# A second set of buffers for k, q and v of every other late pair, and weight sums at other slots

## The chip, the cores and the metric

The kernel runs on one core of a Trainium2 chip. The metric is the device time of one execution in microseconds (us). The kernel before took 863.57 us, the median of three timed runs (862.11 to 866.70). One further execution was profiled; times within the program are from that one and count from the start of its span.

The engines are named as the profile names them: PE multiplies matrices (PEld loads its weights), DVE works on vectors, ACT applies functions and copies, and SP issues nearly all DMAs. Each engine runs its instructions in program order and waits on semaphores for the others.

## The reference

Windowed attention, then a feed-forward layer, all in fp32:

```
q, k, v: [8, 8, 576, 64]                      # batch, heads, sequence, head size
s = (q @ k.T) / 8, masked                     # heads 0-3: the last 32 keys
                                              # heads 4-7: 32 keys, every 4th of the last 128
a = exp(s - max(s));  a = a / (sum(a) + 1e-9)
x = (a @ v), heads side by side               # [4608, 512]: 8 * 576 tokens
h = x @ w_in                                  # [4608, 2048]
g = max(h, 0) + alpha * min(h, 0)
out = g @ w_out                               # [4608, 512]
```

## The kernel before, in words

**Attention.** The 8 x 8 heads are worked as 32 pairs of heads, numbered p = 4 * batch + c; the name 6_1 is batch 6, c = 1, so pair 25. A `Pair` loads k, q and v (L216, L217, L224), multiplies scores on PE (L268), takes row maxima on DVE (L296, L299), exponentials on ACT (L309), divisions and a transpose on DVE (L316 to L324), multiplies values on PE (L286), and copies the result to its place on ACT (L393, `highs`) and DVE (L400, `lows`). Pairs 0 to 19 run in the first 346 us. The twelve late pairs, 20 to 31, run between the matmuls of the paired stage below. Each has one tile for k, one for q and one for v, of which the pool `att` holds one buffer each.

**Feed-forward.** The 4608 tokens are 9 tiles of 512. An fp32 product is made of three products of high and low parts. Tiles 0 to 2 are done singly, early. Tiles 3 to 8 are done two at a time from `paired_stage` (L1109): `phase_h` makes half of h for both tiles by seven block products in place of eight (class `Four`), and `phase_y` (L889) multiplies that half with w_out, in 32 slots of 12 matmuls each (slot n = 8 * column block + row block). A stage is named (t - 3, half): (0, 0) and (0, 1) are tiles 3 and 4, (2, 0) and (2, 1) tiles 5 and 6. Where a stage is listed in `SEVENS` the output product, too, is made of seven block products, which need sums of blocks of w_out.

**Hooks.** What other engines do in a `phase_y` hangs on its slots: a dictionary from slot to operations, which are issued after that slot's matmuls. `attention_hooks` puts pair k of the stage at slots 3 + 5k (scores, the next pair's k and q, maxima, exponentials), 4 later (division, transpose) and 8 later (values, the next pair's v, copies; 7 later for the last). In stage (0, 0) these are pairs 21 to 25; the end of pair 20 is at slot 5.

**Weight sums.** `second_sums` hangs eight sets of sums of w_out blocks on the slots by the table `SUMS`: for each set its number, the slots of its four fetches (256 KB each, from wO into the tiles wy), the slot of its sums on DVE (L1055 and four of L1058), the slot of its parts (a cast on ACT, L1062; a subtraction on DVE, L1063; two stores of 512 KB to wY, L1065, issued by SP), and the pair of buffers. Buffers 1 and 2 hold sets with last entry 1, buffers 3 and 4 those with 3; set 2 thus fetches into the buffers of set 0, and set 7 into those of set 5. Buffers 1 to 4 are also the `stage` tiles of the next `phase_h` (L723, L730).

**Weights.** Every weight block of the paired stage goes through a ring of 10 slots of 256 KB. `feed` (L623) loads the next block each time a slot is used; at every third call it first runs one entry of the list `waiting`, which before the change holds only eight loads of kept tokens. These ring loads, the fetches, the stores, the pairs' loads and the outputs stand in SP's order as the program issues them.

Of the kernel before, what the change touches and what calls it, by code (L numbers as in the profile page):

```python
# [8 lines left out]
F32 = mybir.dt.float32  # L9
# [8 lines left out]
P = 128  # L18
B, H, S, D = 8, 8, 576, 64
# [10 lines left out]
TT = 512  # L30
# [38 lines left out]
def tile_window_attention_prelu_ffn(  # L69
# [12 lines left out]
    nc = tc.nc  # L82
    PS = bass.MemoryType.PSUM

    const = ctx.enter_context(tc.tile_pool(name="const", bufs=1))
# [14 lines left out]
    sums = [const.tile([P, HB], F32, name=f"sums{i}") for i in range(2)]  # L100
# [4 lines left out]
    wY = dram.tile([NFP, 4, P, 2, 2 * P], F32, name="wY")  # L105
    kept = {t: dram.tile([NC, P, TT], F32, name=f"kept_{t}") for t in KEPT}

    turn = {"a": 0, "y": 0, "g": 0, "i": 0, "f": 0}
# [6 lines left out]
    def gbuf(shape, dtype, name, i=None):  # L115
        if i is None:
            i = turn["g"] % 5
            turn["g"] += 1
        return ffp.tile(shape, dtype, tag=f"g{i}", name=name, bufs=1)
# [28 lines left out]
    vsize = (HB + 1) * D  # L148
# [8 lines left out]
    cells = {}  # L157
# [18 lines left out]

    class Pair:
        def __init__(self, b, c):  # L180
            self.b, self.c = b, c
            p = b * NC + c
            self.onto = p <= NC + 1
            self.banks = "y" if self.onto else "a"
            self.late = p == 0
            self.plain = 2 * c < HP
            self.mask = PLAIN if self.plain else DILATED
            self.id = f"{b}_{c}"
            self.pr = spare_pr[p % 2] if b < 2 else pr0
            self.room = rooms[c] if b < 2 else None  # L190
            self.sm = sums[p % 2]
            self.mixed = p >= AHEAD
            self.sides = None
            self.kept = {}

        def target(self, t):
# [11 lines left out]

        def load_qk(self):
            b, c = self.b, self.c  # L210
            if self.room is None:
                self.k = att.tile([P, S], F32, tag="k", name=f"k_{self.id}")
                self.q = att.tile([P, S], F32, tag="q", name=f"q_{self.id}")
            else:
                self.k, self.q = self.room[:, :S], self.room[:, S:2 * S]
            nc.sync.dma_start(out=self.k, in_=kT[b, c])  # L216
            nc.sync.dma_start(out=self.q, in_=qT[b, c])  # L217

        def load_v(self):
            if self.room is None:  # L220
                self.v = att.tile([P, HB + 1 + self.mixed, D], F32, tag="v", name=f"v_{self.id}")
            else:
                self.v = self.room[:, 2 * S:taken].rearrange("p (j d) -> p j d", d=D)
            nc.sync.dma_start(out=self.v, in_=vX[self.b - AHEAD // NC, self.c] if self.mixed else vW[self.b, self.c])  # L224
# [386 lines left out]
    ring, fed, used, waiting = {}, [0], [0], []  # L611
# [10 lines left out]

    def feed():  # L623
        turn["f"] += 1
        if waiting and turn["f"] % 3 == 0:
            waiting.pop(0)()
        if fed[0] < len(units):
            to, u = slot(fed[0]).bitcast(F32), units[fed[0]]
            nc.sync.dma_start(out=to if len(u.shape) == 2 else to.rearrange("p (c n) -> p c n", c=2), in_=u)
            fed[0] += 1  # L630
# [5 lines left out]
    parts, stage = {}, {}  # L636
# [293 lines left out]
    def seven_y(t, grp, us, hooks):  # L930
# [100 lines left out]
                op()  # L1031

    SUMS = {
# [4 lines left out]
    }  # L1038

    def second_sums(hooks, at):  # L1040


        for i, first, then, last, k in SUMS.get(at, ()):
            room = {}

            def fetch(j, i=i, k=k, room=room):
                a, odd = j // 2, j % 2
                if j == 0:
                    room["x"], room["t"] = (gbuf([P, 2, NC, P], F32, f"wy{i}_{n}", k + n) for n in range(2))
                nc.sync.dma_start(  # L1050
                    out=room["xt"[a]][:, odd], in_=wO[i // GP, :, i % GP, :, odd, a].rearrange("c p n -> p c n"))

            def sums(room=room):
                x, t = (room[a].rearrange("p o c n -> p (o c n)") for a in "xt")
                nc.vector.tensor_tensor(out=t, in0=x, in1=t, op=ALU.add)  # L1055
                t = t.rearrange("p (q n) -> p q n", q=4)
                for out, x, y, op in ((3, 1, 3, ALU.add), (1, 0, 1, ALU.subtract), (0, 3, 0, ALU.subtract), (2, 2, 0, ALU.subtract)):
                    nc.vector.tensor_tensor(out=t[:, out], in0=t[:, x], in1=t[:, y], op=op)  # L1058

            def parts(i=i, room=room):  # L1060
                x, t = (room[a].rearrange("p o c n -> p (o c n)") for a in "xt")
                nc.scalar.copy(out=x.bitcast(F32R), in_=t)  # L1062
                nc.vector.tensor_tensor(out=t.bitcast(F32R), in0=t, in1=x, op=ALU.subtract)  # L1063
                for a, w in enumerate((x, t)):
                    nc.sync.dma_start(  # L1065
                        out=wY[i, :, :, a].rearrange("q p n -> p q n"), in_=w.rearrange("p (q n) -> p q n", q=4))

            for j, n in enumerate(first):
                hooks.setdefault(n, []).append(lambda j=j, fetch=fetch: fetch(j))
            for n, op in ((then, sums), (last, parts)):  # L1070
                hooks.setdefault(n, []).append(op)

    def first_scores(u):
        u.scores()
        if u is not pairs[-1]:
            pairs[pairs.index(u) + 1].load_qk()
        u.maxima()

    def begin(u):
# [11 lines left out]
    def end(u):  # L1091
        def op():
            u.values()
            if u is not pairs[-1]:
                pairs[pairs.index(u) + 1].load_v()
            u.highs()
            u.lows()
            u.keep()
        return op
# [9 lines left out]
    def paired_stage():  # L1109
        todo = pairs[AHEAD:]  # L1110
        for u in todo:
            u.banks = "a"
        for t in range(NSTD, NTILE, 2):
            for grp in range(NFP // GP):
                hooks, early = {}, None
# [13 lines left out]
                if t == NSTD:  # L1129
                    early, us, todo = todo[0], todo[1:6], todo[6:]  # L1130
                last = phase_h(t, grp, early=early)[-1]
# [24 lines left out]
    pairs = [Pair(b, c) for b in range(B) for c in range(NC)]  # L1156
# [12 lines left out]
    def conversion():  # L1169

        w = Conversion(*convs.pop(0))
        w.magnitude()
        return w
# [29 lines left out]
    w = conversion()  # L1203
# [5 lines left out]
    before, w = w, conversion()  # L1209
    for s in range(NC):  # L1210
        u = pairs[s]
# [27 lines left out]
        before, w = w, later  # L1239
# [10 lines left out]
    u, v = pairs[NC - 1], pairs[NC]  # L1250
# [70 lines left out]
    for p in range(2 * NC, AHEAD):  # L1321
        n = EARLY + 2 * (p - 2 * NC)
# [5 lines left out]
    for k in range(NFP):  # L1328
        n = SCRATCH + 1 + 2 * k + (2 if k > 1 else 0)
# [89 lines left out]
    feed()  # L1419
    feed()  # L1420
    paired_stage()


# [66 lines left out]
```

## Time and profile before

| what | us |
|---|---|
| median of three runs | 863.57 (862.11 to 866.70) |
| profiled execution | 860.51 |
| its span in the trace | 858.4 |
| PE busy | 838.6 (98%) |
| DVE busy | 615.9 (72%) |
| ACT busy | 433.9 (51%) |
| DMA | 183.48 MB, 214 GB/s over the span |

Busy time is the sum of an engine's instructions. A row of the chain of waits gives a start, a duration and what filled it: an instruction, a DMA on its way, or "issue" where the profile shows nothing that was waited for. A row of a timeline gives start, duration, engine (SPq is SP's queue of DMA issues, with the time to issue and not to land), line, and output and input tile. Granted clock 1.00 is the full TensorE clock.

### The profile page before, as it was taken

The page shows a single profiled execution, that of the slowest core. Times are in us where ns is not written, and L with a number is a line of the kernel's source. Part 1 is how long each engine was busy: PE and PEld are TensorE (multiplying, and loading weights), DVE is VectorE, ACT ScalarE, POOL GpSimd, SP SyncE. Part 2 cuts the span into 40 slices and gives each one's busy share as a digit, 9 for nine tenths or more (in the row PEclk, how much of TensorE's full clock was granted, in tenths as well). Part 3 has the DMA queues.
Part 4 walks back from the last instruction along what each step waited for, and adds up shares of the span by engine and source line. Part 5 has one row for each costly group of instructions (what it writes and reads, how often), then busy time and mean ns, then how long its engine had stood idle before and what let it go on. Part 6 is the DMA issues. An engine that isn't in the chain of part 4 may idle for free.

```text
span 858.4 us, 20273 instructions
## 1 busy us (share of the span) xinstructions
PE 838.6 (98%) x8118; PEld 681.8 (79%) x8118; DVE 615.9 (72%) x1061; ACT 433.9 (51%) x1206; POOL 46.9 (5%) x52
## 2 busy tenths in 40 slices
PE   8789999999999999999999999999999989999998
PEld 5567888888888888887788877888888868888886
DVE  5987767676776768786757788688376758944893
ACT  7885766434344444565437555465265216534640
POOL 0000000200505340000000000000000000000000
PEclk9999999999999999999999999999999999999999
DMA  7743344126989964767987577867886987676664
GB/s 259 266 169 112 138 159 148 44 93 189 293 260 327 314 217 157 237 185 230 304 292 203 176 241 242 269 195 237 257 256 197 286 270 207 191 196 196 191 190 158
DMA packets 133626, 183.48 MB, mean 214 GB/s; under 512 B 10654, under 2 KB 75806, under 8 KB 133534
## 3 DMA queue, kind: packets, MB, share of 16 engines
q1 hardware_dynamic: 133534, 182.20, 67.7%
q8 instruction: 64, 1.05, 0.5%
q14 instruction: 28, 0.23, 0.1%
HBM read 138.12 MB, written 44.04 MB: 212 GB/s over the span
## 4 chain that ended last, share of the span: by engine, by line
PE 91%; DMA 4%; DVE 3%; issue 1%; SPq 0%; ACT 0%; DVEq 0%; ACTq 0%
PE h L466 16%; PE y L514 15%; PE pA L681 15%; PE y L889 11%; PE pC L681 8%; PE qA L1025 7%; PE pB L681 4%; PE qC L1025 4%; PE o L339 3%; PE s L244 2%; PE qB L1025 2%; DMA wy<-wO 2%; PE o L286 1%; PE s L268 1%; DMA w_dt.float<-qT 1%
## 5 line engine op out<-in xcount | busy, mean ns | idle before, releaser
L466 PE MATMUL h<-x,w_dt.float32r 128*128 128x512 f32 x576 | 142.3, 396 | 0.9 <-ACT x L393 0.8
L514 PE MATMUL y<-g,w_dt.float32r 128*128 128x512 f32 x576 | 138.3, 389 | 0.0
L466 PEld LDWEIGHTS h<-x,w_dt.float32r 128*128 128x128 f32 x576 | 107.9, 190 | 24.2 <-ACT x L393 0.9
L514 PEld LDWEIGHTS y<-g,w_dt.float32r 128*128 128x128 f32 x576 | 107.9, 188 | 22.5
L309 ACT ACTIVATE pr<-pr,nm 128x64 f32<-128x64 f32 x216 | 72.3, 337 | 65.6 <-DVE nm L299 65.6
L723 ACT COPY stage<-pA 128x512 f32<-128x512 f32 x72 | 42.0, 584 | 65.9 <-PE pA L681 62.4
L492 ACT CAST g<-m 128x512 fp32r<-128x512 f32 x48 | 29.7, 619 | 74.8 <-DVE m L487 68.7
L681 PE MATMUL pA<-parts_w,ring_w 128*128 128x512 f32 x234 | 58.1, 390 | 3.2 <-ACT stage L723 3.2
L889 PE MATMUL y<-gp,ring_xA 128*128 128x512 f32 x252 | 60.7, 395 | 0.0
L889 PE MATMUL y<-gp,ring_w 128*128 128x512 f32 x240 | 58.2, 394 | 0.0
L681 PE MATMUL pA<-parts_w,ring_xA 128*128 128x512 f32 x234 | 57.8, 389 | 0.0
L889 PEld LDWEIGHTS y<-gp,ring_xA 128*128 128x128 f32 x252 | 46.5, 188 | 10.1
L681 PEld LDWEIGHTS pA<-parts_w,ring_w 128*128 128x128 f32 x234 | 43.8, 188 | 12.7 <-ACT stage L723 3.6
L889 PEld LDWEIGHTS y<-gp,ring_w 128*128 128x128 f32 x240 | 44.3, 188 | 9.6
L681 PEld LDWEIGHTS pA<-parts_w,ring_xA 128*128 128x128 f32 x234 | 43.9, 188 | 9.2
L497 DVE TENSOR_TENSOR g<-m,g 128x512 fp32r<-128x512 f32 x48 | 33.6, 700 | 15.6 <-ACT g L492 15.5
L730 DVE TENSOR_TENSOR stage<-pC,stage 128x512 f32<-128x512 f32 x48 | 33.0, 688 | 12.7 <-ACT stage L723 12.3
L486 DVE TENSOR_SCALAR m<-h,al 128x512 f32<-128x512 f32 x27 | 20.2, 749 | 29.7 <-PE h L466 29.7
L309 ACT ACTIVATION_READ_ACCUMULATOR pr<-pr,nm 128x1 f32 x216 | 40.7, 188 | 0.0
L730 DVE TENSOR_TENSOR stage<-pB,stage 128x512 f32<-128x512 f32 x24 | 16.5, 689 | 31.1 <-PE pB L681 31.1
L741 DVE SCALAR_TENSOR_TENSOR n<-n,bal,stage 128x512 f32<-128x512 f32 x36 | 27.0, 749 | 7.9 <-ACT n L737 7.3
L749 DVE TENSOR_TENSOR gp<-n,gp 128x512 fp32r<-128x512 f32 x48 | 31.5, 682 | 0.0
(196 smaller groups left out, 1540.0 us busy)
## 6 DMA issues: line engine op xcount, KB each, us to landing
ring_xA<-wS SPq DMA_DIRECT2D x66, 256.0 KB, 3.1
ring_w<-wS SPq DMA_DIRECT2D x65, 256.0 KB, 3.2
ring_g<-wS SPq DMA_DIRECT2D x37, 256.0 KB, 3.6
ring_xA<-wO SPq DMA_DIRECT2D x36, 256.0 KB, 3.1
ring_w<-wO SPq DMA_DIRECT2D x36, 256.0 KB, 3.1
wO<-w_dt.float32r SPq DMA_DIRECT2D x32, 256.0 KB, 4.2
wS<-wc SPq DMA_DIRECT2D x16, 512.0 KB, 4.4
wy<-wO SPq DMA_DIRECT2D x32, 256.0 KB, 5.6
```

Source lines behind the costliest of these rows:

```text
L309: nc.scalar.activation(out=self.pr[:, r, :], in_=self.ps[r // CUT0][:, r % CUT0, :] if self.onto else self.pr[:, r, :], func=AF.Exp, bias= ...
L466: nc.tensor.matmul(ms[t, f], lhsT=weight(0, a, f)[:, c * P:(c + 1) * P], rhs=half(t, c)[:, e, :], start=(c == 0 and n == 0), stop=(c == NC ...
L492: nc.scalar.copy(out=g[:, 0, :], in_=ms[t, f])
L497: nc.vector.tensor_tensor(out=g[:, 1, :], in0=ms.pop((t, f)), in1=g[:, 0, :].bitcast(F32), op=ALU.subtract)
L514: nc.tensor.matmul(ys[t][c], lhsT=weight(1, a, f)[:, c * P:(c + 1) * P], rhs=g[:, e, :], start=(first and n == 0), stop=(last and n == 2),)
L681: nc.tensor.matmul(to, lhsT=w[:, (2 * a + c) * P:(2 * a + c + 1) * P], rhs=part_of(name, e)[:, c * TT:(c + 1) * TT], start=start and c == ...
L723: nc.scalar.copy(out=self.s(n), in_=self.A)
L730: nc.vector.tensor_tensor(out=self.s(n), in0=getattr(self, src), in1=self.s(to), op=ALU.add)
L741: nc.vector.scalar_tensor_tensor(out=self.m[n], in0=self.m[n], scalar=bal[:, f:f + 1], in1=self.at(n), op0=ALU.mult, op1=ALU.add)
L749: nc.vector.tensor_tensor(out=g[:, 1], in0=self.m.pop(n), in1=g[:, 0].bitcast(F32), op=ALU.subtract)
L889: nc.tensor.matmul(ys2[tt], lhsT=w[:, k * P:(k + 1) * P], rhs=g[:, e], start=j == 0 and n == 0, stop=j == GF - 1 and n == 2)
L1025: nc.tensor.matmul(to(q)[c], lhsT=w[:, k * P:(k + 1) * P], rhs=rhs[:, e], start=(i, q) in firsts and n == 0, stop=i == GP - 1 and n == 2, ...
```

## The change

Pairs 21, 23, 25, 27, 29 and 31 (odd and late) keep k, q and v in a second place, the tile `second_room`, which takes the memory tagged xB1. With two places, a pair's k and q are issued after the scores of the pair two before it instead of one, and its v after the values of the pair two before. The loads of pair 21 are put into `waiting`, of which `feed` now takes one at every second call.

In `SUMS`, six of the eight sets have another slot for something: sets 1, 2, 6 and 7 fetch, sum and cast sooner, sets 3 and 5 move one operation, sets 0 and 4 keep theirs. The two stores of every set are taken out of `parts` and issued one slot (high parts) and two slots (low parts) after it.

```diff
@@ -176,6 +176,11 @@
 
 
 
+    def second_room():
+        if "pairs" not in cells:
+            cells["pairs"] = const.tile([P, 4 * TT], F32, tag="xB1", name="second_room")
+        return cells["pairs"]
+
     class Pair:
         def __init__(self, b, c):
             self.b, self.c = b, c
@@ -191,6 +196,7 @@
             self.sm = sums[p % 2]
             self.mixed = p >= AHEAD
             self.sides = None
+            self.other = self.mixed and p % 2 == 1
             self.kept = {}
 
         def target(self, t):
@@ -208,7 +214,9 @@
 
         def load_qk(self):
             b, c = self.b, self.c
-            if self.room is None:
+            if self.other:
+                self.k, self.q = second_room()[:, :S], second_room()[:, S:2 * S]
+            elif self.room is None:
                 self.k = att.tile([P, S], F32, tag="k", name=f"k_{self.id}")
                 self.q = att.tile([P, S], F32, tag="q", name=f"q_{self.id}")
             else:
@@ -217,7 +225,9 @@
             nc.sync.dma_start(out=self.q, in_=qT[b, c])
 
         def load_v(self):
-            if self.room is None:
+            if self.other:
+                self.v = second_room()[:, 2 * S:2 * S + vsize + D].rearrange("p (j d) -> p j d", d=D)
+            elif self.room is None:
                 self.v = att.tile([P, HB + 1 + self.mixed, D], F32, tag="v", name=f"v_{self.id}")
             else:
                 self.v = self.room[:, 2 * S:taken].rearrange("p (j d) -> p j d", d=D)
@@ -622,7 +632,7 @@
 
     def feed():
         turn["f"] += 1
-        if waiting and turn["f"] % 3 == 0:
+        if waiting and turn["f"] % 2 == 0:
             waiting.pop(0)()
         if fed[0] < len(units):
             to, u = slot(fed[0]).bitcast(F32), units[fed[0]]
@@ -1031,10 +1041,10 @@
                 op()
 
     SUMS = {
-        (0, 0): ((0, (4, 5, 6, 7), 9, 12, 1), (1, (10, 11, 12, 14), 19, 22, 3), (2, (16, 17, 19, 20), 24, 29, 1)),
-        (0, 1): ((3, (14, 15, 16, 19), 24, 29, 1),),
+        (0, 0): ((0, (4, 5, 6, 7), 9, 12, 1), (1, (9, 10, 11, 12), 15, 17, 3), (2, (16, 17, 18, 19), 21, 25, 1)),
+        (0, 1): ((3, (14, 15, 16, 19), 24, 27, 1),),
         (2, 0): ((4, (8, 9, 10, 11), 16, 19, 1),),
-        (2, 1): ((5, (3, 4, 5, 6), 9, 13, 1), (6, (11, 12, 13, 14), 18, 21, 3), (7, (19, 20, 21, 22), 26, 29, 1)),
+        (2, 1): ((5, (3, 4, 5, 6), 10, 13, 1), (6, (7, 8, 9, 10), 15, 18, 3), (7, (17, 18, 19, 20), 22, 25, 1)),
     }
 
     def second_sums(hooks, at):
@@ -1061,19 +1071,21 @@
                 x, t = (room[a].rearrange("p o c n -> p (o c n)") for a in "xt")
                 nc.scalar.copy(out=x.bitcast(F32R), in_=t)
                 nc.vector.tensor_tensor(out=t.bitcast(F32R), in0=t, in1=x, op=ALU.subtract)
-                for a, w in enumerate((x, t)):
-                    nc.sync.dma_start(
-                        out=wY[i, :, :, a].rearrange("q p n -> p q n"), in_=w.rearrange("p (q n) -> p q n", q=4))
+
+            def store(a, i=i, room=room):
+                w = room["xt"[a]].rearrange("p o c n -> p (o c n)")
+                nc.sync.dma_start(
+                    out=wY[i, :, :, a].rearrange("q p n -> p q n"), in_=w.rearrange("p (q n) -> p q n", q=4))
 
             for j, n in enumerate(first):
                 hooks.setdefault(n, []).append(lambda j=j, fetch=fetch: fetch(j))
-            for n, op in ((then, sums), (last, parts)):
+            for n, op in ((then, sums), (last, parts), (last + 1, lambda store=store: store(0)), (last + 2, lambda store=store: store(1))):
                 hooks.setdefault(n, []).append(op)
 
     def first_scores(u):
         u.scores()
-        if u is not pairs[-1]:
-            pairs[pairs.index(u) + 1].load_qk()
+        for v in pairs[pairs.index(u) + 2:][:1]:
+            v.load_qk()
         u.maxima()
 
     def begin(u):
@@ -1091,8 +1103,8 @@
     def end(u):
         def op():
             u.values()
-            if u is not pairs[-1]:
-                pairs[pairs.index(u) + 1].load_v()
+            for v in pairs[pairs.index(u) + 2:][:1]:
+                v.load_v()
             u.highs()
             u.lows()
             u.keep()
@@ -1110,6 +1122,7 @@
         todo = pairs[AHEAD:]
         for u in todo:
             u.banks = "a"
+        waiting.extend((todo[1].load_qk, todo[1].load_v))
         for t in range(NSTD, NTILE, 2):
             for grp in range(NFP // GP):
                 hooks, early = {}, None
```

DVE in stage (0, 0), around the division of pair 24 (6_0) and the maxima of pair 25 (6_1); wy1 and wy2 are the buffers of sets 1 and 2, rs and pr belong to a pair's division, pt to its transpose. Before:

```order
L316 TENSOR_SCALAR rs_6_0_5404<-sums0_79 128x9
L317 RECIPROCAL rs_6_0_5404<-rs_6_0_5404 128x9
L318 TENSOR_TENSOR pr0_78<-pr0_78,rs_6_0_5404 128x576
L324 STREAM_TRANSPOSE pt_6_0_5408<-pr0_78 128x576
L1063 TENSOR_TENSOR wy1_1_5007<-wy1_1_5007,wy1_0_5006 128x1024
L296 SCALAR_TENSOR_TENSOR pr0_78<-s_6_1_0_5421,mask_sb_74 128x320
L299 TENSOR_REDUCE nm_6_1_5463<-pr0_78 128x5
L296 SCALAR_TENSOR_TENSOR pr0_78<-s_6_1_1_5422,mask_sb_74 128x256
L299 TENSOR_REDUCE nm_6_1_5463<-pr0_78 128x4
L907 COPY py_1_4922<-y_3_0_2_1_5167 128x512
L1055 TENSOR_TENSOR wy2_1_5234<-wy2_0_5233,wy2_1_5234 128x1024
L1058 TENSOR_TENSOR wy2_1_5234<-wy2_1_5234 128x256 x4
```

After:

```order
L1065 TENSOR_TENSOR wy2_1_5238<-wy2_0_5237,wy2_1_5238 128x1024
L1068 TENSOR_TENSOR wy2_1_5238<-wy2_1_5238 128x256 x4
L326 TENSOR_SCALAR rs_6_0_5411<-sums0_79 128x9
L327 RECIPROCAL rs_6_0_5411<-rs_6_0_5411 128x9
L328 TENSOR_TENSOR pr0_78<-pr0_78,rs_6_0_5411 128x576
L334 STREAM_TRANSPOSE pt_6_0_5415<-pr0_78 128x576
L306 SCALAR_TENSOR_TENSOR pr0_78<-s_6_1_0_5424,mask_sb_74 128x320
L309 TENSOR_REDUCE nm_6_1_5464<-pr0_78 128x5
L306 SCALAR_TENSOR_TENSOR pr0_78<-s_6_1_1_5425,mask_sb_74 128x256
L309 TENSOR_REDUCE nm_6_1_5464<-pr0_78 128x4
L917 COPY py_1_4924<-y_3_0_2_1_5171 128x512
L1073 TENSOR_TENSOR wy2_1_5238<-wy2_1_5238,wy2_0_5237 128x1024
```

The sums of set 2 (L1055 and L1058, now L1065 and L1068) stood behind the maxima of pair 25 and now stand ahead of the division of pair 24; the low parts of set 1 (L1063) are gone from here to an earlier place, and those of set 2 (L1073) follow pair 25's maxima.

SP in the same stage, from the fetches of set 2 on; 5_3 is pair 23, 6_2 pair 26, ring is a weight block. Before:

```order
L1050 DMA wy2_0_5233<-wO_83 128x4x128
L629 DMA ring_xA1_4244<-wS_82 128x512
L1050 DMA wy2_0_5233<-wO_83 128x4x128
L216 DMA k_6_1_5294<-kT 128x576
L217 DMA q_6_1_5295<-qT 128x576
L629 DMA ring_xA1_4244<-wS_82 128x512
L1050 DMA wy2_1_5234<-wO_83 128x4x128 x2
L629 DMA ring_g0_4360<-wS_82 128x512
L224 DMA v_6_0_5385<-vX 128x704
L1065 DMA wY_85<-wy1_0_5006 128x4x256
L1065 DMA wY_85<-wy1_1_5007 128x4x256
```

After:

```order
L1060 DMA wy2_0_5237<-wO_83 128x4x128
L639 DMA ring_xA1_4244<-wS_82 128x512
L1060 DMA wy2_0_5237<-wO_83 128x4x128
L224 DMA k_6_2_5300<-kT 128x576
L225 DMA q_6_2_5301<-qT 128x576
L1077 DMA wY_85<-wy1_0_5002 128x4x256
L1060 DMA wy2_1_5238<-wO_83 128x4x128
L639 DMA ring_xA1_4244<-wS_82 128x512
L1077 DMA wY_85<-wy1_1_5003 128x4x256
L1060 DMA wy2_1_5238<-wO_83 128x4x128
L639 DMA ring_g0_4360<-wS_82 128x512
L234 DMA second_room_4427<-vX 128x704
```

Between the second fetch of set 2 into wy2_0 and its last into wy2_1 now stand the loads of pair 26 and both stores of set 1; before, the loads of pair 25 stood there, and the stores came after.

SP in stage (2, 1), from the fetches of set 7 on; ob_5_2 are the two outputs of the third column block. Before:

```order
L1065 DMA wY_85<-wy6_0_7984 128x4x256
L1065 DMA wY_85<-wy6_1_7985 128x4x256
L1050 DMA wy7_1_8068<-wO_83 128x4x128 x2
L629 DMA ring_w3_1_4113<-wS_82 128x512
L913 DMA out<-ob_5_2_0_8107 128x512
L913 DMA out<-ob_5_2_1_8110 128x512
L629 DMA ring_xA1_4244<-wS_82 128x512 x3
L1065 DMA wY_85<-wy7_0_8067 128x4x256
L1065 DMA wY_85<-wy7_1_8068 128x4x256
```

After:

```order
L1060 DMA wy7_1_8036<-wO_83 128x4x128
L1077 DMA wY_85<-wy6_1_7927 128x4x256
L1060 DMA wy7_1_8036<-wO_83 128x4x128
L639 DMA ring_w3_1_4113<-wS_82 128x512 x2
L923 DMA out<-ob_5_2_0_8095 128x512
L923 DMA out<-ob_5_2_1_8098 128x512
L639 DMA ring_xA1_4244<-wS_82 128x512
L1077 DMA wY_85<-wy7_0_8035 128x4x256
L639 DMA ring_xA1_4244<-wS_82 128x512
L1077 DMA wY_85<-wy7_1_8036 128x4x256
```

The first store of set 7 (wy7_0) still stands behind the outputs of the third column block; it is now behind one ring load after them instead of three, and the low-part store follows after one more.

## Rows read from the trace of the kernel before

**Rows 1.** Waits of PE, 340 to 858 us: waiter, releaser, us, times, longest.

```profile
PE pA L681 <- ACT stage L723: 3.2, 1, 3.2
PE s L268 <- issue: 0.9, 1, 0.9
PE s L268 <- DMA q<-qT: 0.3, 1, 0.3
```

**Rows 2.** Stages (0, 0) and (2, 1): length, busy, granted clock, DMA share, GB/s.

```profile
382.80:444.00 61.20, 59.99 (x1069) 47.63 (x1068) 41.72 (x91) 28.97 (x128) 0.00 (x0) 1.00 0.84 261
652.00:704.20 52.20, 48.98 (x217) 40.22 (x216) 36.44 (x47) 15.84 (x20) 0.00 (x0) 1.00 0.78 244
```

**Rows 3.** Chain of waits, 405 to 445 us: start, us, what.

```profile
413.49 5.37 DMA q<-qT
```

**Rows 4.** DVE, stage (0, 0): start, us, engine, line, output, input.

```profile
422.87 1.22 DVE L1055 TENSOR_TENSOR wy<-wy,wy 128x1024 f32<-128x1024 f32 x1
424.12 1.80 DVE L1058 TENSOR_TENSOR wy<-wy 128x256 f32<-128x256 f32 x4
...
427.13 0.16 DVE L316 TENSOR_SCALAR rs<-sums 128x9 f32<-128x9 f32 x1
...
429.09 1.18 DVE L1063 TENSOR_TENSOR wy<-wy,wy 128x1024 fp32r<-128x1024 f32 x1
430.35 0.49 DVE L296 SCALAR_TENSOR_TENSOR pr<-s,mask_sb 128x320 f32<-128x320 f32 x1
...
435.75 0.52 DVE L400 COPY kept<-o 128x160 f32<-128x160 f32 x2
436.19 0.17 DVE L316 TENSOR_SCALAR rs<-sums 128x9 f32<-128x9 f32 x1
```

**Rows 5.** ACT in time, stage (0, 0).

```profile
431.45 0.35 ACT L309 ACTIVATE pr<-pr,nm 128x64 f32<-128x64 f32 x1 [3.34 <-DVE nm L299]
...
434.46 0.56 ACT L909 COPY py<-y 128x512 f32<-128x512 f32 x1
...
436.10 1.07 ACT L1062 CAST wy<-wy 128x1024 fp32r<-128x1024 f32 x1
```

**Rows 6.** PE in time, stage (0, 0): the values of pair 25.

```profile
441.30 1.13 PE L286 MATMUL o<-pt,v 32*64 32x32 f32 x84
```

**Rows 7.** SP in time, stage (0, 0): fetches of set 2.

```profile
417.71 0.43 SPq L1050 DMA_DIRECT2D wy<-wO  x1
...
423.08 0.98 SPq L1050 DMA_DIRECT2D wy<-wO  x2
```

**Rows 8.** DMA issues, 417.6 to 418.2 us: KB each, median us to landing.

```profile
wy<-wO SPq DMA_DIRECT2D x1, 256.0 KB, 6.6
```

**Rows 9.** DMA while set 2 is fetched: columns as in rows 2.

```profile
418.00:424.00 6.00, 4.79 (x88) 3.59 (x88) 3.21 (x6) 1.74 (x11) 0.00 (x0) 1.00 1.08 344
424.00:430.00 6.00, 6.00 (x171) 4.68 (x170) 5.17 (x15) 3.01 (x16) 0.00 (x0) 1.00 0.92 292
```

**Rows 10.** Tile wy, 390 to 446 us.

```profile
DMA to landing us min/median/max: 3.7/5.1/6.7
```

**Rows 11.** Chain of waits, 640 to 710 us.

```profile
690.89 5.20 DMA wy<-wO
...
700.42 3.01 DMA wY<-wy
703.53 0.59 ACT stage L723
```

**Rows 12.** DVE, stage (2, 1): the outputs of a column block.

```profile
690.95 1.28 DVE L912 TENSOR_TENSOR ob<-y,py 128x512 f32<-128x512 f32 x2
```

**Rows 13.** An early stretch with a lower clock: columns as in rows 2.

```profile
48.00:50.00 2.00, 0.96 (x46) 0.86 (x49) 1.93 (x5) 1.35 (x6) 0.00 (x0) 1.00 1.04 385
50.00:52.00 2.00, 2.00 (x46) 1.71 (x39) 1.97 (x4) 2.00 (x13) 0.00 (x0) 0.60 0.84 341
52.00:54.00 2.00, 2.00 (x6) 1.53 (x5) 1.93 (x8) 1.14 (x8) 0.00 (x0) 0.55 0.51 164
```

## The prediction

> **What bounds the kernel now.** I read the page's busy shares first, then the list of what the matmul engine (PE) waited for, then the table of stages, and then the chain of waits and the single engines around the two places where PE stood still. PE is the bound: from 340 us to the end, which holds every stage that the change touches, it waits three times, 3.2, 0.9 and 0.3 us, 4.4 us in all [rows 1]. So the change can win at most those 4.4 us, and it can lose whatever it makes late by more than PE's work in between. All three waits lie in two stages: 61.20 us with 59.99 us of PE work, and 52.20 us with 48.98 us [rows 2]. The first stage is the output product of tiles 3 and 4, first half (call it A); it runs pairs 21 to 25 of the attention and weight sums 0 to 2 between its matmuls. The second is the output product of tiles 5 and 6, second half (B), with weight sums 5 to 7.
>
> In A the wait is for pair 24's q, issued at 413.49 and 5.37 us under way [rows 3]. In B it is for the store of set 7's high parts: the buffer holding it is wanted by a copy that PE waits for [rows 11].
>
> **Term 1, loads a pair sooner.** k and q of pair 24 are now issued right after the scores of pair 22 instead of 23, about five slots (7 us) earlier in SP's order, so they land well before 418.9. The wait for them, 0.33 us, goes. The 0.88 us that stand as "issue" after 60 of the 72 score matmuls follow directly on that late landing, and in none of the other pairs' scores in this stretch does the list show one [rows 1]; I count them with it: -1.2 us, with ends of -0.3 (the 0.88 is something else) and -1.2. The other loads were never waited for, so they are worth nothing; the 8 loads of kept tokens and pair 21's loads are issued at every second turn of the weight ring instead of every third, behind matmuls that wait for nothing there [rows 1].
>
> **Term 2, set 2's sums in front of pair 24's division.** This is what I expect to decide. DVE runs in program order. Before, the sums of set 2 stood behind the maxima of pair 25; now they stand in front of the division of pair 24, and DVE cannot pass them while it waits for set 2's last fetch. Behind them in the new order: pair 24's division and transpose (needed by its value matmuls on PE), pair 25's maxima, its exponentials on ACT, one copy and set 2's cast there, set 2's low parts on DVE, pair 24's copies, and the division of pair 25, which PE needs for pair 25's values.
>
> That chain, with the durations of before [rows 4, 5]: sums 422.87 to 425.92, 3.05; division and transpose 427.13 to 429.09, 1.96; maxima until ACT can begin, 430.35 to 431.45, 1.10; exponentials 431.45 to 434.46, 3.01; copy 0.56; cast 1.07; low parts 1.18; pair 24's copies 435.75 to 436.19, 0.44; division and transpose 1.96. Sum 14.33 us. PE reached pair 25's values at 441.30 [rows 6], and with term 1 gone it would at 440.1. So the sums must start by 440.1 - 14.3 = 425.8, or PE is late by the difference, first at pair 24's values, the rest at pair 25's.
>
> When does the last fetch of set 2 land? Its second fetch was issued at 417.71 and took 6.6 us, so it landed at 424.3 [rows 7, 8]; it stands at the same slots in the new order. After it in the queue come, by the new order of SP: k and q of pair 26 (288 KB each), the high-part store of set 1 (512), the third fetch (256), a ring block (256), the low-part store of set 1 (512) and the fourth fetch (256): 2368 KB, or 2.425 MB. Before, k and q of pair 25, the third fetch and a ring block stood there, and no store. The DMA engines were saturated then: 344 GB/s at a share of 1.08, and 292 GB/s in the next 6 us [rows 9]. At 344 GB/s the data take 7.05 us: 424.3 + 7.1 = 431.4. The sums then start 5.6 us late: +5.6 us, about half of it in front of pair 24's values.
>
> Ends: if the queue ahead counted for nothing, the fetch would be issued at its old place, 423.08 plus half a us, less one slot (1.36 us) for its earlier hook, and take the shortest landing of this stretch, 3.7 us [rows 7, 10]: 425.9, a lag of 0.1. At 292 GB/s it lands at 432.6: 6.8. I take 5.6, because the rows for exactly this queue show 344 GB/s. The Trainium skill (DMA: Bandwidth & Descriptors, section "Anatomy of one DMA — SWDGE (gpsimd) path") gives a transfer about 2.0 us fixed plus its bytes at 436 GB/s, 2.6 us for such a fetch as an estimate, and has no term for what is queued ahead; by it the lag would be about nothing, and the 6.6 us row speaks against it here.
>
> **Term 3, set 7's store in B.** The fetches of set 7 are two slots (2.7 us) sooner. Its last one landed at 690.89 + 5.20 = 696.1 [rows 11]; now at about 693.4, so that the sums end at 693.4 + 3.05 = 696.5 and the cast at 697.6. But SP sends the store only after the outputs of the third column block, and these are now formed on DVE behind the sums and one low part: 696.5 + 1.2 for the low part (as 1.18 in [rows 4]) + 1.28 = 699.0 [rows 12], then two output DMAs and a ring block, 0.3 to 0.4 us each to issue: the store leaves at about 699.8, against 700.42. In front of it in the queue are now 768 KB just issued, with its own 512 KB 1.31 MB, at the 292 to 344 GB/s of rows 9 3.8 to 4.5 us: landing at 703.6 to 704.3, against 703.5 before. Value +0.4; ends -3.2 (the store leaves right after the cast and takes 3.01 us as before, so the copy waits for nothing) and +1.5 (5.2 us like the fetch, 705.0). The gain that earlier sums bring is eaten by the outputs that now wait behind them.
>
> **Terms at nothing.** Sets 3, 4, 5 and 6 move by one to four slots; PE waited for none of them, and the DVE work is the same in number. If a set in another stage were to wait as set 2 does, it would cost the same way; none has two loads and two stores in the few slots before its sums.
>
> **Sum.** -1.2 + 5.6 + 0.4 = +4.8 us. The profiled execution took 860.51 us, so 865.3 in a profile; the median of the three timed runs is 863.57, 3.1 higher, and I put the forecast on that: 868.4 us.
>
> **Rivals.** (a) Other side: the queue does not hold set 2's fetch up and the store of set 7 leaves at once. It needs the sums of set 2 to start by 425.8, 5.6 us earlier than I reckon, and the store to be issued by 700.2 minus its 3.2 us wait. Price: -1.2 + 0.1 - 3.2 = -4.3, 859.3 us. For it: one fetch did land in 3.7 us [rows 10]; against it: the fetch one place before it took 6.6 [rows 8] with less in front. That page's rule would bring the first half of it. Chance 0.12; with only the first half, -0.7, 862.9, counted in (b).
> (b) Partial lag: the stores to HBM leave more quickly than fetches land, or SP is held back so that fewer bytes stand ahead, and the fetch lands at 426 to 429.5. Lag 0.2 to 3.7, sum -0.6 to +2.9: 863 to 866.5, middle 865. Chance 0.22.
> (c) The forecast, 866.5 to 870: 0.43.
> (d) The forecast and a slower clock after it. In 50 to 54 us the granted clock was 0.60 and 0.55, a mix of its two levels 1.2 and 2.4 GHz, after PE had been busy for 0.96 of the 2 us before [rows 13]; 4 us of full PE at those levels lose 2 x 0.40 + 2 x 0.45 = 1.7 us. If PE's wait for pair 24 brings that once: 870.1 us; twice 871.8. Against it: the 3.2 us of waiting in B left the stage's clock at 1.00 [rows 2]. The Trainium skill (TensorE: Matmul & The Clock Gate, section "HAM oscillation — how this bites in real kernels") says that waits for DMA between bursts of matmuls let the clock gate fall, and that the next burst starts cold; the case here would be the wait of 3 to 5 us in A. Chance 0.18.
> (e) The second room is not free when pair 21 needs it, since it takes the memory of a token tile that was still being read: SP would stand before the ring's loads, and PE would wait for weights in a stage that now shows no wait. Price up to the 5.37 us of one load in flight, 874 us. Chance 0.05.
>
> **How the numbers follow.** A measurement here tells about 0.5%, 4.3 us, from no change: faster means under 859.3, slower over 867.9. Case (a) lies on the first border, half of it beyond; with a little for things not seen that gives faster 0.09. Slower: most of (c), which straddles the border at 866.5 to 870 (0.28 of its 0.43), all of (d) and (e): 0.51. The rest, 0.40, is no change that can be told. Range: 860 to 872.5 us; it leaves out the better part of (a), the end of (d) and (e), about 0.2 in all.
>
> **What would show it.** Right: DVE idle in front of the sums of set 2 with a DMA of wO as releaser, for 3 us or more; PE waiting at the value matmuls of pairs 24 and 25 for the transpose, 4 to 7 us together; no wait at the scores of pair 24; the copy in B still waiting some 3 us for the store. Wrong: sums of set 2 that start before 427, or a store of set 7 issued within a us of its cast. The step I trust least is the rate at which 2.4 MB drain before the fourth fetch.

## The result and the profile after

The changed kernel takes 868.42 us (median of 20 runs), the kernel before 862.2 us over as many; the ratio is 1.0078, 95% interval 1.0062 to 1.0094. It is slower, by 6.2 us between the medians and 5.3 to 8.1 us by the interval; 868.4 had been forecast. The forecast added 4.8 us to 863.57, the median of three runs; over 20 runs the kernel before is 1.4 us quicker than that, so the difference came out larger than forecast while the time came out as forecast. The profiled execution took 867.39 us, 6.9 more than the one before.

What PE waited for, 340 us to the end of the changed kernel (waiter, releaser, us, times, longest):

```profile
PE pA L691 <- ACT stage L733: 3.4, 1, 3.4
PE o L296 <- DVE pt L334: 2.5, 1, 2.5
PE o L296 <- DVE pr L306: 0.8, 2, 0.6
PE s L278 <- issue: 0.4, 1, 0.4
```

The wait for q [rows 1] is gone. In its place PE waits 2.5 us for pair 24's transpose (L334) and 0.8 us for the maxima of pair 25 (L306), which share their score banks with pair 24's outputs. The wait for the copy in stage (2, 1) has stayed.

DVE in stage (0, 0): the sums of set 2 and the transposes of pairs 24 and 25.

```profile
430.66 1.22 DVE L1065 TENSOR_TENSOR wy<-wy,wy 128x1024 f32<-128x1024 f32 x1 [4.81 <-DMA ring_g<-wS]
...
434.88 0.78 DVE L334 STREAM_TRANSPOSE pt<-pr 128x576 f32<-128x576 f32 x1
...
444.23 0.78 DVE L334 STREAM_TRANSPOSE pt<-pr 128x576 f32<-128x576 f32 x1
```

The sums start at 430.66, after 4.81 us of standing still, and the chain that was added up ahead of the run follows: pair 25's transpose ends at 445.01, 14.35 us after the start of the sums, where 14.33 had been added up. PE would have wanted it at 439.9: before, pair 25's values came 15.96 us after those of pair 23 (425.34 to 441.30 [rows 6]), and here pair 23's start at 423.91. The first of these lines is of the kernel before, the second of the changed one:

```profile
425.34 1.13 PE L286 MATMUL o<-pt,v 32*64 32x32 f32 x84
```

```profile
423.91 1.13 PE L296 MATMUL o<-pt,second_room 32*64 32x32 f32 x84
```

The releaser of DVE's wait is given as a ring load. That load was issued 0.75 us behind the last fetch and, by the list of DMA issues, landed 6.9 us later, at 431.8, when the sums had begun; the sums read only the fetches. So the wait is taken to be for the last fetch, whose own landing the trace does not give. SP shows the fetches and what was put among them:

```profile
418.36 0.43 SPq L1060 DMA_DIRECT2D wy<-wO  x1
419.72 0.33 SPq L224 DMA_DIRECT2D k<-kT  x1
420.10 0.43 SPq L225 DMA_DIRECT2D q<-qT  x1
420.62 0.38 SPq L1077 DMA_DIRECT2D wY<-wy  x1
421.05 0.50 SPq L1060 DMA_DIRECT2D wy<-wO  x1
...
423.40 0.72 SPq L1077 DMA_DIRECT2D wY<-wy  x1
424.17 0.66 SPq L1060 DMA_DIRECT2D wy<-wO  x1
```

The last fetch leaves at 424.17, 6.5 us before the sums begin, behind the loads of pair 26 and both stores of set 1. The DMA engines were full from then on, at 376 GB/s, a little quicker than the 344 of [rows 9]:

```profile
424.00:431.00 7.00, 7.00 (x178) 5.71 (x179) 1.12 (x6) 1.86 (x14) 0.00 (x0) 1.00 1.08 376
```

PE in the same stage: values of pair 24, the matmuls behind them, values of pair 25.

```profile
435.72 0.30 PE L296 MATMUL o<-pt,v 32*64 32x32 f32 x4 [2.53 <-DVE pt L334]
...
437.17 1.46 PE L296 MATMUL o<-pt,v 32*64 32x32 f32 x78 [0.56 <-DVE pr L306]
438.56 8.02 PE L899 MATMUL y<-gp,ring_w 128*128 128x512 f32 x24
446.50 1.12 PE L296 MATMUL o<-pt,second_room 32*64 32x32 f32 x84
```

Between the two value groups stand 24 matmuls of the same form and number as before: four slots of six, for a slot has six matmuls in the kernel, and not the twelve that its description above gives. They take 8.02 us here and took 5.73 us in the kernel before:

```profile
435.64 5.73 PE L889 MATMUL y<-gp,ring_w 128*128 128x512 f32 x24
```

The stages (length, busy time per engine, granted clock, DMA share, GB/s) say why:

```profile
433.00:436.00 3.00, 0.47 (x5) 0.19 (x4) 2.76 (x7) 0.00 (x0) 0.00 (x0) 1.00 0.32 110
436.00:438.00 2.00, 1.15 (x60) 1.02 (x64) 1.93 (x5) 1.13 (x7) 0.00 (x0) 0.66 0.00 0
438.00:440.00 2.00, 2.00 (x46) 1.65 (x35) 0.16 (x1) 2.00 (x13) 0.00 (x0) 0.50 0.23 50
440.00:442.00 2.00, 2.00 (x6) 1.61 (x5) 0.59 (x1) 1.78 (x5) 0.00 (x0) 0.50 0.40 138
```

The granted clock is 0.66 and then 0.50, 1.2 GHz, from 436 on, right after the stretch in which PE was busy for 0.47 of 3 us. So PE never saw the wait for pair 25's transpose: the slow matmuls lasted 1.5 us beyond it.

Stage (2, 1), the chain of waits and the same columns around it:

```profile
704.88 3.84 DMA wY<-wy
...
708.82 0.59 ACT stage L733
```

```profile
706.00:709.40 3.40, 0.04 (x1) 0.00 (x0) 1.39 (x3) 0.58 (x1) 0.00 (x0) 1.00 1.01 358
709.40:711.00 1.60, 1.54 (x4) 1.24 (x5) 0.00 (x0) 0.01 (x1) 0.00 (x0) 0.59 1.00 341
711.00:713.00 2.00, 2.00 (x6) 1.51 (x6) 0.00 (x0) 0.59 (x1) 0.00 (x0) 0.50 1.04 395
```

The store of set 7 leaves at 704.88 and lands at 708.72; shifted by the 5.1 us that PE is late, it leaves 0.6 us sooner than before [rows 11] and lands 0.2 us later. After this 3.4 us wait the clock is 0.50 to 0.59. After the 3.2 us of [rows 1] it had stayed at 1.00 in the profile before; the stretch of [rows 2] ends with that wait, and this row follows it:

```profile
704.20:708.00 3.80, 3.80 (x17) 3.13 (x18) 0.69 (x1) 0.59 (x1) 0.00 (x0) 1.00 1.01 333
```

Where PE stands against the profile before, at the same instructions, gives the balance: 414.60 to 414.10 at the values of pair 22, -0.5 us (0.3 of it by 346 us already, ahead of all that the change touches); 425.34 to 423.91 at those of pair 23, another -0.9 across the scores of pair 24; 435.64 to 438.56 behind pair 24's values, +4.3; 441.30 to 446.50 at pair 25's values, +2.3 in the 24 matmuls; 704.17 to 709.46 behind the wait in (2, 1), +0.1; 707.04 to 713.91 two products on, +1.6. Together +6.9.

### The profile page after: what moved, and what is told of

Its sections match the earlier page's. It is cut to its first block, busy times and chain, and to the rows that moved or that the text cites. A ratio compares the mean times of both kernels' runs of the same rounds, so it can differ in the third digit from the quotient of the medians.

```text
span 865.3 us, 20274 instructions
## 1 busy us (share of the span) xinstructions
PE 841.5 (97%) x8118; PEld 684.2 (79%) x8118; DVE 615.8 (71%) x1061; ACT 433.9 (50%) x1206; POOL 47.0 (5%) x52
## 4 chain that ended last, share of the span: by engine, by line
PE 93%; DVE 2%; DMA 2%; ACT 1%; issue 1%; SPq 0%; DVEq 0%; ACTq 0%
PE h L476 15%; PE pA L691 15%; PE y L524 15%; PE y L899 15%; PE pC L691 7%; PE qA L1035 7%; PE pB L691 4%; PE qC L1035 4%; PE o L349 3%; PE s L254 2%; PE qB L1035 2%; PE o L296 1%; PE s L278 1%; DMA ws<-w_in 1%; DMA ring_g<-wS 1%
## 5 line engine op out<-in xcount | busy, mean ns | idle before, releaser
L899 PE MATMUL y<-gp,ring_w 128*128 128x512 f32 x240 | 60.3, 405 | 0.0
```

The lines of the kernel that those rows point to most:

```text
L899: nc.tensor.matmul(ys2[tt], lhsT=w[:, k * P:(k + 1) * P], rhs=g[:, e], start=j == 0 and n == 0, stop=j == GF - 1 and n == 2)
```

## The experiments

All ratios are to the kernel before, on the same chip. The diffs show the changed entries, and `...` stands for what is left out. The theory was that the loss comes from set 2's sums in front of pair 24's division, with the fetch late behind its queue, and from the clock after the waits.

**Only the loads.** Changed kernel with the table and the stores of before:

```diff
-        (0, 0): (..., (1, (9, 10, 11, 12), 15, 17, 3), (2, (16, 17, 18, 19), 21, 25, 1)),
+        (0, 0): (..., (1, (10, 11, 12, 14), 19, 22, 3), (2, (16, 17, 19, 20), 24, 29, 1)),
...
```

> Only the pair loads of the change: second room, loads two pairs ahead, pair 21 through the weight ring's list; weight sums and their stores at the slots of before. Theory (the loss comes from the sums of set 2 standing ahead of pair 24's division): no wait of PE in stage (0, 0) but at most the 0.4 us of issue at the scores of pair 24, stage (2, 1) as before with its 3.2 us wait, clock 1.00 in both; 0.9 us less than before, ratio 0.997 to 1.001. Rival (the loads that now run ahead fill the DMA queue and hold up what others wait for): PE waits of some us in stage (0, 0), ratio 1.004 to 1.008.

Measured 862.12 us, ratio 0.9998 (0.9976 to 1.0019). Waits of PE, and the clock in stage (2, 1):

```profile
PE pA L691 <- ACT stage L733: 3.5, 1, 3.5
PE s L278 <- issue: 1.2, 1, 1.2
```

```profile
697.70:701.20 3.50, 0.06 (x1) 0.00 (x0) 2.23 (x3) 0.59 (x1) 0.00 (x0) 0.84 0.81 270
701.20:704.00 2.80, 2.76 (x7) 2.18 (x8) 0.00 (x0) 0.00 (x0) 0.00 (x0) 0.50 0.95 326
```

No wait in the stage but 1.2 us of "issue" at pair 24's scores. So the loads cost nothing and, with the q wait gone, win nothing that can be measured. The "issue" is not the late q: it stays, at 0.3 to 1.5 us and after 60 or 61 of the same 72 matmuls, in the list of every kernel run here but one (set 1's stores moved). Stage (2, 1) has the slots of before in this kernel, and here too the clock falls to 0.50 after the wait: the profile before happened to keep it.

**Only the sums.** Kernel before with the new table and the separate stores.

```diff
-        (0, 0): (..., (2, (16, 17, 19, 20), 24, 29, 1)),
+        (0, 0): (..., (2, (16, 17, 18, 19), 21, 25, 1)),
...
-            for n, op in ((then, sums), (last, parts)):
+            for n, op in ((then, sums), (last, parts), (last + 1, lambda store=store: store(0)), ...
```

> Only the new slots of the weight sums and the separate stores; pairs load one ahead into one place as before. Theory: the last fetch of set 2 still stands behind 2.4 MB of loads and stores, DVE waits 4 to 5 us for it, PE 3 to 4 us at the values of pair 24, then a granted clock near 0.5 for some us; with the scores of pair 24 still waiting for q, 7 to 8 us more than before, ratio 1.008 to 1.010. Rival (the loads are the cause): ratio 0.998 to 1.002, no wait at the values of pair 24.

Measured 869.27 us, ratio 1.0079 (1.0053 to 1.0105), the whole loss. Waits of PE:

```profile
PE pA L681 <- ACT stage L723: 4.8, 1, 4.8
PE o L286 <- DVE pt L324: 3.0, 1, 3.0
PE s L268 <- issue: 0.9, 1, 0.9
PE o L286 <- DVE pr L296: 0.6, 2, 0.4
```

The transpose and the maxima are waited for as in the changed kernel. The loads are cleared. The ratio lies just under the 1.008 to 1.010 that were expected, and what was expected of q did not come: no wait for it stands here, though the pairs load as in the kernel before.

**Set 2's sums back.** Changed kernel, one entry:

```diff
-(2, (16, 17, 18, 19), 21, 25, 1)
+(2, (16, 17, 18, 19), 24, 29, 1)
```

> The changed kernel with the sums and the parts of set 2 back at slots 24 and 29, its fetches and all else as changed. Theory: DVE waits for nothing ahead of pair 24's division, PE has no wait at its values, the clock stays at 1.00 in stage (0, 0); stage (2, 1) still costs 0.2 us of wait and about 1.6 us of clock: about 1 us more than before, ratio 0.999 to 1.003. Rival (loads and stores crowd the queue and PE waits for something else in the stage): 4 us or more, ratio over 1.005.

Measured 863.58 us, ratio 1.0014 (0.9994 to 1.0035): 5.5 us of the loss hang on this entry. Waits of PE, and the columns of the stages behind pair 24's values and after the wait in (2, 1):

```profile
PE pA L691 <- ACT stage L733: 5.9, 2, 4.7
PE s L278 <- issue: 0.9, 1, 0.9
```

```profile
431.00:438.00 7.00, 7.00 (x130) 5.61 (x132) 4.67 (x10) 2.06 (x7) 0.00 (x0) 1.00 0.63 182
703.50:708.00 4.50, 4.47 (x11) 3.55 (x12) 0.00 (x0) 0.59 (x1) 0.00 (x0) 0.54 1.04 380
```

Clock 1.00 where it was 0.50. Two waits remain for the copies: 4.7 us in (2, 1), and a new one of 1.2 us at the start of the stage after (0, 0). There the copy waits for set 2's first store, which by the chain of waits leaves at 440.81, behind the store of pair 25's kept rows (L213) that it preceded before, and lands at 444.82. The wait in (2, 1) is 1.5 us longer than before, where 0.2 had been expected.

**Set 1's stores behind the last fetch.** Changed kernel:

```diff
-(last + 1, lambda store=store: store(0)), (last + 2, lambda store=store: store(1))
+(last + (3 if i == 1 else 1), lambda store=store: store(0)), (last + (4 if i == 1 else 2), lambda store=store: store(1))
```

> The changed kernel with the two stores of set 1 two slots later, behind the last fetch of set 2. Theory (the fetch is late by what is queued ahead of it): 1 MB less stands ahead, 3.0 us at 344 GB/s, so the sums of set 2 start near 427.7 us instead of 430.7, PE waits under 1 us at the values of pair 24 and about 2 us at those of pair 25; with stage (2, 1) as changed about 3 us more than before, ratio 1.002 to 1.005. Rival (the fetch is late because it is issued late, or its own time is 6 us whatever is ahead): sums still at 430 or later, ratio 1.007 to 1.009.

Measured 863.71 us, ratio 1.0026 (1.0004 to 1.0049). DVE's sums of set 2, then PE's matmuls between the two value groups and its wait at pair 25:

```profile
429.14 1.23 DVE L1065 TENSOR_TENSOR wy<-wy,wy 128x1024 f32<-128x1024 f32 x1 [2.29 <-issue]
```

```profile
436.62 5.73 PE L899 MATMUL y<-gp,ring_w 128*128 128x512 f32 x24
443.59 1.10 PE L296 MATMUL o<-pt,second_room 32*64 32x32 f32 x84 [1.24 <-issue]
```

In this execution PE ran 1.0 us later at the values of pair 23 than in the changed kernel (424.90 against 423.91), and had been 1.3 us late by 346 us already, so the sums at 429.14 stand 2.5 us sooner, against 3.0 expected from 1 MB at 344 GB/s. The wait at pair 24's values shrank to 0.8 us, the clock stayed full and the 24 matmuls took 5.73 us; then PE waited 1.24 us for pair 25's transpose, which ended at 443.49. So the two stores in front of the fetch cost 2.5 us of its lateness; the rest of what stood in front was not moved.

One half of the rival stays open. The fetch left at 422.65, with PE's 1.0 us taken off 2.5 us sooner than in the changed kernel, and by the list of DMA issues it still took 6.4 us to land. So the delay shows in when SP issued the fetch, and the run does not tell "bytes in front over the rate" from "some 6.4 us once it is issued in this stretch".

**Matmuls that compute nothing in the waits.** Changed kernel, with work for PE ahead of pair 24's values and of the product that waits in (2, 1):

```diff
+FILL_A, FILL_B = 36, 13
...
+            if self.id == "6_0":
+                g = gpart(0, 0)
+                for _ in range(FILL_A):
+                    nc.tensor.matmul(self.po[0].rearrange("p n q -> p (n q)"), lhsT=g[:, 0, :P], rhs=g[:, 0, :CUT0 * BQ], ...)
...
-            if q in (1, 2, 7):
+            if q == 6 and self.id == "7_0_0":
+                self.bank("B")
+                for _ in range(FILL_B):
+                    nc.tensor.matmul(self.B, lhsT=part_of("B11", 0)[:, :P], rhs=part_of("B11", 0)[:, :TT], ...)
+            if q in (1, 2, 7) and not (q == 2 and self.id == "7_0_0"):
```

> The changed kernel with matmuls that compute nothing in the two places where PE waits: 36 of 160 columns into pair 24's output bank ahead of its values (about 2.6 us), 13 of 512 columns into an unused bank ahead of the product that waits for the copy in the stage after (2, 1) (about 3 us). Theory (the waits cost again by a lower clock after them): the sums of set 2 and the store of set 7 come as late as in the changed kernel, but the granted clock stays at 1.00 behind both places, the 24 matmuls after pair 24's values take 5.7 us instead of 8.0, PE then waits some 1 to 1.5 us for pair 25's transpose; 2 to 3 us less than the changed kernel, ratio to before 1.004 to 1.006. Rival (those matmuls are slow for another reason, such as weights or buffers that come late): 8.0 us as before and a ratio of 1.007 to 1.009.

Measured 866.48 us, ratio 1.0047 (1.0021 to 1.0073): by the ratios 2.7 us less than the changed kernel, though the two intervals overlap. The data came as late: the sums of set 2 start 6.9 us after pair 23's values (431.84 and 424.93), against 6.75 in the changed kernel. PE in stage (0, 0), then the stages' columns:

```profile
434.04 4.14 PE L289 MATMUL o<-gp 128*128 128x160 f32 x36
...
439.32 5.73 PE L910 MATMUL y<-gp,ring_w 128*128 128x512 f32 x24
446.29 1.17 PE L302 MATMUL o<-pt,second_room 32*64 32x32 f32 x84 [1.24 <-issue]
```

```profile
434.00:438.10 4.10, 4.10 (x37) 3.99 (x36) 3.80 (x9) 0.04 (x1) 0.00 (x0) 1.00 0.26 86
438.10:445.00 6.90, 6.90 (x109) 5.57 (x108) 3.54 (x9) 4.87 (x23) 0.00 (x0) 1.00 0.18 52
710.20:713.00 2.80, 2.73 (x12) 2.26 (x13) 0.00 (x0) 0.60 (x2) 0.00 (x0) 1.00 1.06 383
```

The filling took 4.14 us instead of 2.6, longer than the wait it covered. Still the clock stays at 1.00 at both places, the 24 matmuls take 5.73 us, and PE waits 1.2 us for pair 25's transpose. The weight loads were busy for 3.99 of these 4.1 us, so they are likely to have set the pace of the filling. The clock was thus a cost of its own. Its size is less sure: from pair 23's values to two products behind the wait in (2, 1) this profile is 1.8 us shorter than the changed kernel's, and the medians say 2.7, both with a filling that was itself too long.

**Other buffers for sets 5 to 7.** Kernel before, last entry of the three sets:

```diff
-(5, (3, 4, 5, 6), 9, 13, 1), (6, (11, 12, 13, 14), 18, 21, 3), (7, (19, 20, 21, 22), 26, 29, 1)
+(5, (3, 4, 5, 6), 9, 13, 3), (6, (11, 12, 13, 14), 18, 21, 1), (7, (19, 20, 21, 22), 26, 29, 3)
```

> The kernel before with one edit: sets 5, 6 and 7 change places in the buffers (3 and 4, 1 and 2, 3 and 4), so that the store of set 7 reads a buffer that the next stage's copies want some 5 us later. Theory (PE's 3.2 us wait in stage (2, 1) is for that buffer alone): the wait goes, and with it the lower clock that follows it in some runs; 3.2 to 5 us less, ratio 0.994 to 0.997. Rival (the buffers 3 and 4 come free late, so the fetches of set 5 hold SP, or the copy then waits for the outputs' or low parts' work): within 1 us of before, ratio 0.999 to 1.001.

Measured 856.82 us, ratio 0.9937 (0.9917 to 0.9956). The only wait of PE left, and the stage around the copy:

```profile
PE s L268 <- issue: 1.5, 1, 1.5
```

```profile
697.60:705.00 7.40, 7.40 (x33) 5.89 (x33) 4.03 (x6) 3.27 (x6) 0.00 (x0) 1.00 0.75 251
```

5.4 us less for a wait of 3.2 to 3.5, a little more than expected. The rest fits the clock that followed the wait in many executions: the median of the mean granted clock is 0.9975 in these ten and 0.995 in the kernel before, which over 857 us is 2.1 us by an estimate; no run takes the two apart. This kernel is quicker than both; the two that follow cannot be told apart from it.

**Both.** Changed kernel with the table and the stores of before, as in the first experiment, and those buffers:

```diff
-        (2, 1): ((5, (3, 4, 5, 6), 10, 13, 1), (6, (7, 8, 9, 10), 15, 18, 3), (7, (17, 18, 19, 20), 22, 25, 1)),
+        (2, 1): ((5, (3, 4, 5, 6), 9, 13, 3), (6, (11, 12, 13, 14), 18, 21, 1), (7, (19, 20, 21, 22), 26, 29, 3)),
...
```

> The pair loads of the change, the weight sums at the slots of before, and sets 5, 6 and 7 with changed buffers. Theory: the gains add: 0.3 us of q wait and 3.2 to 5 us of the store's wait; ratio 0.993 to 0.997. Rival: the loads a pair sooner take DMA time from the other, ratio over 0.998.

Measured 858.42 us, ratio 0.9948 (0.9927 to 0.9968). The loads add nothing that can be measured to the buffers: the intervals of the two kernels overlap. That the gains add, as had been expected, is not shown.

**Set 7's store ahead of the outputs.** Set 2 back as above, and set 7's parts before the third column block's outputs:

```diff
-(7, (17, 18, 19, 20), 22, 25, 1)
+(7, (17, 18, 19, 20), 22, 23, 1)
-(last + 1, lambda store=store: store(0)), (last + 2, lambda store=store: store(1))
+(last + (i != 7), lambda store=store: store(0)), (last + 1 + (i != 7), lambda store=store: store(1))
```

> The changed kernel with set 2's sums and parts at slots 24 and 29, and set 7's parts at slot 23 with its stores at 23 and 24, so that DVE's low parts and SP's high-part store stand ahead of the outputs of the third column block. Theory (the gain of earlier sums in stage (2, 1) was eaten by these outputs): the store leaves within 0.5 us of its cast, about 3 us sooner than in the same kernel with the parts at 25 where PE waited 4.7 us; PE waits 0 to 2 us there, ratio to before 0.996 to 0.999. Rival (the store's own time in a busy queue decides): wait still 3 us or more, ratio 1.000 to 1.003.

Measured 857.12 us, ratio 0.9950 (0.9929 to 0.9971). The chain of waits at the store:

```profile
699.27 1.06 ACT wy L1072
...
700.35 2.98 DMA wY<-wy
...
703.44 0.59 ACT stage L733
```

The store leaves as the cast ends, where it had left 2.2 us after it with the parts at slot 25, and it takes 2.98 us instead of 3.98. PE waits 1.4 us instead of 4.7, and the time is a little better than expected. So the earlier sums did bring the data sooner (the cast starts 3.5 us ahead of PE's wait, at 699.27 against 702.72, where it was 1.6 us before), and the outputs and the ring block in front of the store had eaten it.

## Why the prediction was right, step by step

The forecast of slower by 4.8 us stood on one step, and that step held: set 2's sums in front of pair 24's division, with the last fetch late behind 2.4 MB. The fetch was put at 431.4 and had landed by 430.66; the lag by the chain was put at 5.6 and came out at 5.1 (445.0 against 439.9). The entry put back removes it, the stores moved behind the fetch shorten it, and the sums alone reproduce the whole loss. Why the fetch is late is shown in part: the two stores cost 2.5 us of it, and bytes over the rate, which the forecast went by, is one reading of the rest.

The rule of the Trainium skill (DMA: Bandwidth & Descriptors, section "Anatomy of one DMA — SWDGE (gpsimd) path") gives such a fetch about 2.6 us, an estimate from a fit for DMAs that GpSimd issues. This one was issued by SP and the sums began 6.5 us after it, so the rival that leaned on that rule is out.

Not all the signs came as they were written. The wait of DVE (4.81 us), the missing wait for q and the wait for the copy (3.4 us) did, though the profile names a ring load and not a load of wO as DVE's releaser. The 4 to 7 us of waiting at the values of pairs 24 and 25 did not: PE waited 3.3 us at pair 24's, and at pair 25's it waited for nothing, because slow matmuls filled that time.

That is rival (d), which came true on top of the forecast. It had been given a chance of 0.18, with the clock of stage (2, 1) in the profile before as the point against it. That point was weak: the row named for it ends where the wait ends, and one execution kept the clock after it while the 3.5 us wait of the loads-only kernel lost it. The price was right: 1.7 us each time was forecast, and in the changed kernel the clock cost 1.5 us beyond the chain in (0, 0) and 1.6 us in (2, 1). With both, the forecast would have been about 8 us slower by the profile. The medians lie only 6.2 us apart; that executions of the kernel before lose the clock too would explain it, but no run shows how much.

The Trainium skill (TensorE: Matmul & The Clock Gate, section "HAM oscillation — how this bites in real kernels") says that matmuls after a wait for DMA start cold. The trace agrees in the changed kernel, where the matmuls after the 3.4 us wait in (2, 1) ran at 0.50 to 0.59, and not in the profile before, where those after 3.2 us ran at 1.00.

Term 1 was mis-sized: 1.2 us were expected of the loads, with the 0.88 us of "issue" in them, and these stay without the late load. At most the 0.33 us of waiting for q were theirs, and that wait is gone in the kernel with the sums alone too. What the "issue" is the runs don't settle; in the three profiles looked at (before, changed, loads only) an instruction DMA of 16 KB runs 1 to 3 us ahead of the gap.

Term 3 was right in kind and too small: +0.4 was taken between -3.2 and +1.5. PE's wait in (2, 1) was 3.4 us in the changed kernel's profile but 4.7 to 4.9 in the three others with the same slots, so +1.5 was the price in three profiles of four. In all four the store left 2.2 us after its cast, behind the outputs; what differs is the cast, which started 4.4 us ahead of PE's wait in the first and 2.9 to 3.2 us in the others. The cost that was put at nothing had one hole: the separate store of set 2 made the next stage's copy wait 1.2 us once the rest was out of the way.

Rival (a) did not happen, since the fetch was late and the store too. Rival (b) did not, the sums starting after 429.5. Rival (e) did not: PE has no wait for the second room.

That the forecast came so close to 868.42 is partly luck, from two errors that cancel: the three runs of before lay 1.4 us above the later median, and the clock was left out of the sum.

## What to carry to other kernels

Before an operation is moved ahead on an engine that runs in order, ask when its data land by the queue in front of the fetch (here the bytes over the measured rate came within 0.8 us), and add up what stands behind it until the bound engine needs it. A wait of the matmul engine, such as the 3.4 us here, may be charged a second time by its clock, which one profile can hide; look at the mean clock of several executions. Where a buffer is wanted early by the next stage, give the last user another buffer: three changed digits took 5.4 us off, where the moved slots and loads had cost 6.2.

## What the runs showed that was not expected

The mean granted clock of whole executions lay between 0.987 and 0.994 in the changed kernel's 20, between 0.990 and 1.000 in 32 of the kernel before, and between 0.996 and 1.000 in the ten with the other buffers. The 32 took 856 to 867 us, and the longer ones are those with the lower clock (correlation -0.80). The wait in (2, 1) is not the only place where it falls: between 50 and 54 us, far ahead of the change, the profile before has 0.60 and 0.55 [rows 13] and that of the changed kernel 1.00. Where the unprofiled executions lost it is not shown.

Matmuls of 160 columns took 115 ns each (36 in 4.14 us), where 512 columns take 227 ns (6 in 1.36 us), so a third of the columns took half the time. The weight loads ahead of the short ones were busy throughout, at 111 ns each, which would explain their pace; no run varied the loads alone.
